# The last chunk's inverse butterflies reordered and written to other tiles, the third layer's normalisation split in two, and the butterfly scratch tile moved

## The chip, the cores and the metric

The kernel runs as one program on one core of a Trainium2 chip. The metric is the device time of one execution in microseconds; the figure before is the median of three executions. A profiled execution of the same program, taken separately, gives the trace.

## The reference

Four layers are applied to `x` of 2048 rows (time) by 640 columns (channels), each behind a layer norm without weights and each added to `x`:

```python
x = A_u
x = x + _A_ref(_layernorm(x), A_re, A_im, B_re, B_im, C_re, C_im, log_dt, Dskip)   # layer "a"
x = x + _B_ref(_layernorm(x), wq, wk, wv, wo)                                     # layer "b"
x = x + _A_ref(_layernorm(x), A_re, ...)                                          # layer "c"
x = x + _B_ref(_layernorm(x), wq, ...)                                            # layer "d"
```

`_A_ref` is a long convolution: a kernel of 2048 taps for each channel is built from complex exponentials, and the convolution is done by FFT over 4096 points, product and inverse FFT, plus a skip term. `_B_ref` is attention with 32 query heads of 20 columns and one shared key and value head, softmax over 2048 keys, and an output projection.

## The kernel before, in words

`tile_layers` (L1351) runs the parts in order: `kgen` builds the convolution's taps and stores them in DRAM (`kd`); `conv_layer("a", True)`, `attn_layer("b")`, `conv_layer("c", False)`, `attn_layer("d", out)`. The activations `x` stay in SBUF as 16 tiles `tau` = 0 to 15 of 128 rows and 640 columns. The engines are TensorE (PE), ScalarE (ACT), VectorE (DVE), GpSimd (POOL) and SyncE (SP, which issues most DMAs); each works through its own queue in order.

**A convolution layer.** The 640 channels are cut into five chunks `c` of 128. For one chunk the work is:

- `normals` or `normal` (L760 to L770): ACT writes the normalised chunk into the tile `xn`, one instruction of 128x128 for each `tau` and copy. `norm` (L694, with `rstd` and `root`) works the scales and shifts out of the mean and variance in `mv`: some ten tiny DVE instructions around one square root on ACT.
- `raw` (L562) or `dense` (L594): PE multiplies by the tables `wf`. There are four groups `t` of 128-wide products, each into its own PSUM tile `z`, and ACT copies each into the chunk's spectrum tile `A` (16 slots of 256 columns). `dense` does a first butterfly inside the products, by a moving operand of 256 columns and by negated copies in `xn` (24 ACT instructions instead of 16). With `raw` this first butterfly is left to DVE: `halve` (L580), two instructions of 128x2048. `halved` (L820) says how many chunks go by `raw`: one in layer a, two in layer c.
- `fft8` (L104): the forward butterflies, 16 DVE instructions between `A` and the scratch tile `B`.
- The product with the taps' spectrum `kh`: `spread` (L840), eight DVE instructions and four accumulating DMAs issued by POOL; for the last chunk `product` (L778), six DVE instructions with the scratch `R`. `load_spectrum` (L709) fetches `kh` by a DMA on SP's queue.
- `halve` and `fft8` again for the inverse, then `inverse` (L792): PE multiplies the slots by the tables `wi`, in four groups `g` of four `tau` each, group `g` holding the `tau` with `tau % 4 == FIRST[g]`, `FIRST = (0, 2, 1, 3)`. `residual` (L810) adds the result to `x`, on DVE or, for chunks 0 and 3, on ACT. The results `y` go through two PSUM banks in turn, so the third group waits until the first one's residual has read its bank; `turn` (L899) issues residual `g` and then `inverse` `g + 2`.

Chunks overlap: while DVE does one chunk's inverse, PE prepares the one after the next. Inside `conv_layer` the order on PE, ACT and DVE is the order in which the code is written (`manual_schedule`), and `weave` puts pieces of one list between the pieces of another. In layer a, `kernel_spectra` (L718) first runs the five chunks of taps through `raw`, `whole` and a store to `kh`. In layer a's last chunk, pieces of `attn_weights` (L928) on ACT and PE are woven between the DVE instructions. Then `stats_last` and `norm_part` finish the norm for the attention layer that follows.

**An attention layer.** `_attn` (L997) normalises `x`, transposes it and makes queries, keys and values; `main_loop` (L1150) goes through 4 x 8 x 16 steps of scores (L1187), exponentials on ACT (L1191) and values (L1201). Output projections are slipped in between (L1261), their sums into `x` and the statistics for the next norm done on DVE (`add`, `stats`). After the last step `normalize_last` (L1234) makes the tile `on`, and the last projections of the last four `tau` (all with `tau % 4 == 3`) use it with the weights `wol` (L1307). Here the order on PE and ACT is written by hand, that on DVE is left to the planner.

**Where tiles lie.** A pool gives each tile its place by the order of creation. The convolution's pool, the pools of an attention layer and `kgen`'s pool start at the same address, right behind `x` and its small companions. So a tile may only be written once the last reader of whatever lay there before is done. In KiB from that start: `kgen`'s two staging tiles `kst`, from which the taps are stored to DRAM, lie at 0 to 16. In the convolution pool, `B` is created in `conv_setup` and lies at 0 to 16, `R` at 16 to 24. In layer c `xn` lies at 24 to 36, `A1` at 36 to 52, `kh` at 52 to 68, `wi` from 68. An attention layer's pools have `kt`, `vt` and others at 0 to 15, the query tiles at 15 to 27, `wo` at 27 to 40, `wol` at 40 to 42, the exponentials `pt` at 42 to 66, two tiles `on` at 66 to 70, and the projection's staging tiles `ot` at 74 to 94.

Of the kernel before, what the change touches and what calls it, by code (L numbers as in the profile page):

```python
# [21 lines left out]
P = 128  # L22
# [124 lines left out]

def weave(calls, between):

    for i in range(len(calls) + 1):  # L150
        for n, call in between:
            if n == i or (i == len(calls) and n > i):
                call()
        if i < len(calls):
            calls[i]()


class Net:
# [7 lines left out]
    def setup(self, ctx):  # L166
# [8 lines left out]
        self.mv = self.xp.tile([P, 16, 2], F32, name="mv")  # L175
# [355 lines left out]
    def conv_setup(self, ctx):  # L531
# [3 lines left out]
        self.cvp = ctx.enter_context(tc.tile_pool(name="cvp", bufs=1, reuse_waits="tile"))  # L535

        self.B = self.cvp.tile([P, 16, 256], F32, name="B")
# [20 lines left out]
    def spectrum(self, nm, k):  # L558
        tag = f"A{k}" if k < 3 else "kh"
        return self.cvp.tile([P, 16, 256], F32, tag=tag, bufs=1, name=f"A{nm}")  # L560

    def raw(self, xn, nm, k):  # L562
# [4 lines left out]
        for t in range(4):  # L567
# [12 lines left out]
    def halve(self, A, pieces=1):  # L580
# [3 lines left out]
        for i in range(pieces):  # L584
# [5 lines left out]
    def whole(self, A, sg, pieces=1):  # L590

        return self.halve(A, pieces) + fft8(self.nc, A, self.B, sg, low=self.B[:, 8:16])
# [32 lines left out]
    def stats(self, t):  # L625
# [5 lines left out]
        nc.vector.bn_aggr(self.mv[:, t], st.rearrange("p a b -> p (a b)"))  # L631
# [62 lines left out]
    def norm(self, nm):  # L694
        rs = self.xp.tile([P, 16], F32, tag="rs", bufs=2, name=f"rs{nm}")
        nmr = self.xp.tile([P, 16], F32, tag="nmr", bufs=2, name=f"nmr{nm}")
        self.rstd(self.xp, self.mv, rs, nmr, 16)
        return rs, nmr

    def rstd(self, pool, mv, out, nmr, n):  # L700

        nc = self.nc
        ve = pool.tile([P, n], F32, tag="ve", bufs=2, name="ve")
        sq = pool.tile([P, n], F32, tag="sq", bufs=2, name="sq")
        nc.vector.tensor_scalar(ve, mv[:, :, 1], EPS, None, ALU.add)
        self.root(ve, sq, out)
        nc.vector.scalar_tensor_tensor(nmr, mv[:, :, 0], -1.0, out, op0=ALU.mult, op1=ALU.mult)
# [10 lines left out]
    def kernel_spectra(self):  # L718
# [5 lines left out]
        ktl = cv.tile([P, 24, DC], F32, tag="xn", name="ktl")  # L724
        ks += [kts[:, c] for c in range(3)] + [ktl[:, 0:16]]
# [12 lines left out]
    def conv_layer(self, nm, first):  # L738
# [4 lines left out]
        B = self.B  # L743
        tt = nc.vector.tensor_tensor
        with tc.manual_schedule(engines={mybir.EngineType.PE, mybir.EngineType.Activation,
                                         mybir.EngineType.DVE}):
            rs, nmr = self.norm(nm)
            rsm = self.xp.tile([P, 16], F32, tag="rsm", bufs=1, name=f"rsm{nm}")
# [644 lines left out]
```

## Time and profile before

| what | us |
|---|---|
| median of 3 executions (3016.51 to 3018.91) | 3018.55 |
| profiled execution, its own time | 3015.11 |
| its span in the trace | 3013.3 |
| layer a, first product with the taps to last product (L574 to L804) | 301.2 to 613.8 |
| attention b, first scores to last projection (L1187 to L1261) | 734.2 to 1692.8 |
| layer c, first normalising instruction to last product (L761 to L804) | 1698.3 to 1927.9 |
| attention d, first scores (L1187) | 2048.1 |

A row of the timeline gives start, duration, engine, line and operation, the tiles (written <- read, buffer numbers left out, so `Ak` are the spectra of the taps, `Aa` and `Ac` those of layers a and c), the count of merged instructions, and in brackets how long the engine had stood idle and who ended that. A row of the windows gives for each stretch its length, the busy time of PE, weight loads, DVE, ACT and POOL with instruction counts, then PE's granted clock as a share of full speed, the DMA share and GB/s. A row of the waits gives who waited for whom: total us, times, longest. The chain that ended last covers only attention d, so the stages around the change are read from timelines.

### The profile page before, as it was taken

Reading aid. Unit: us, or ns where it says so; the run is one execution under the profiler, and the core shown is the slowest. Engines: PE = TensorE matmul, PEld = TensorE weight load, DVE = VectorE, ACT = ScalarE, POOL = GpSimd, SP = SyncE. Lnnn points to the kernel's source line nnn. Section 1 sums busy time; section 2 is a strip of 40 time slices with the busy share of each in tenths; the row PEclk is TensorE's granted clock in tenths of the full one; section 3 lists DMA queues with packets and bytes.
Section 4 is the critical chain, followed back from the end, with each engine's and each line's share of the span. In section 5 each row is a group of like instructions: output and inputs, shape, how many; then the busy total and the mean of one; then the engine's idle time right before and its main releaser. Section 6 shows DMA issues by size and latency. Waiting matters only on the chain. (4 is left out here: it accounts for less than half of the span.)

```text
span 3013.3 us, 52501 instructions
## 1 busy us (share of the span) xinstructions
PE 2787.7 (93%) x21712; PEld 1275.9 (42%) x21712; DVE 1371.8 (46%) x1774; ACT 2429.1 (81%) x2910; POOL 86.6 (3%) x149
## 2 busy tenths in 40 slices
PE   2776999898999999999999898798999999999999
PEld 0333988775232323333333687673223333333323
DVE  7999899942122232322232499721222223232222
ACT  5888343444999999999999534238999999999997
POOL 0001001000000000000000011000000000000000
PEclk9855999999999999999999999899999999999999
DMA  6113555433200000100000256131000100110100
GB/s 145 34 21 106 170 168 112 103 114 112 81 22 25 22 27 20 28 23 24 25 22 20 87 112 152 35 131 56 24 25 22 43 22 26 38 28 22 42 19 23
DMA packets 126001, 175.60 MB, mean 58 GB/s; under 512 B 59461, under 2 KB 81989, under 8 KB 122133
## 3 DMA queue, kind: packets, MB, share of 16 engines
q1 hardware_dynamic: 102680, 137.70, 15.8%
q0 software_dynamic: 21104, 33.45, 5.5%
q8 instruction: 175, 2.87, 0.4%
q10 hardware_dynamic: 1968, 0.98, 0.1%
q14 instruction: 74, 0.60, 0.1%
HBM read 95.22 MB, written 48.04 MB: 48 GB/s over the span
## 5 line engine op out<-in xcount | busy, mean ns | idle before, releaser
L1191 ACT ACTIVATE pt<-scb 128x1024 f32<-128x1024 f32 x1024 | 942.1, 1120 | 7.0 <-PE scb L1187 5.7
L1191 ACT ACTIVATE pt<-scd 128x1024 f32<-128x1024 f32 x1024 | 942.2, 1117 | 6.3 <-PE scd L1187 4.9
L1201 PE MATMUL pod<-pt,vt 128*32 128x512 f32 x4096 | 546.5, 606 | 4.4 <-DVE on L1218 0.5
L1201 PE MATMUL pob<-pt,vt 128*32 128x512 f32 x4096 | 546.4, 605 | 4.4 <-DVE on L1218 0.5
L1187 PE MATMUL scb<-qpb,kt 62*128 62x512 f32 x2048 | 385.6, 451 | 6.6 <-PEq L1136 5.9
L1187 PE MATMUL scd<-qpd,kt 62*128 62x512 f32 x2048 | 385.7, 451 | 5.8 <-DVEq L1136 5.4
L1187 PEld LDWEIGHTS scb<-qpb,kt 62*128 62x128 f32 x2048 | 166.1, 185 | 402.2 <-ACT pt L1191 392.3
L1187 PEld LDWEIGHTS scd<-qpd,kt 62*128 62x128 f32 x2048 | 166.0, 185 | 401.3 <-ACT pt L1191 391.9
L1249 DVE TENSOR_TENSOR x<-pyd,x 128x320 f32<-128x320 f32 x146 | 71.8, 492 | 560.8 <-PE pyd L1261 560.8
L1249 DVE TENSOR_TENSOR x<-pyb,x 128x320 f32<-128x320 f32 x146 | 71.8, 492 | 547.4 <-PE pyb L1261 547.4
L1221 DVE RECIPROCAL rc<-rc 128x512 f32<-128x512 f32 x62 | 207.9, 3353 | 2.1
L1201 PEld LDWEIGHTS pod<-pt,vt 128*32 128x32 f32 x4096 | 80.6, 108 | 177.9 <-issue 159.9
L1201 PEld LDWEIGHTS pob<-pt,vt 128*32 128x32 f32 x4096 | 80.6, 108 | 177.5 <-issue 159.5
L608 PE MATMUL za<-xna,wf 128*128 128x256 f32 x512 | 114.0, 384 | 7.7 <-ACT xna L761 7.7
L608 PEld LDWEIGHTS za<-xna,wf 128*128 128x128 f32 x512 | 97.9, 192 | 23.1 <-ACT xna L761 9.7
L1261 PE MATMUL pyb<-wo,ot 128*32 128x320 f32 x1168 | 105.3, 432 | 0.0
L1261 PE MATMUL pyd<-wo,ot 128*32 128x320 f32 x1168 | 105.3, 432 | 0.0
L804 PE MATMUL yc<-Ac,wi 128*128 128x128 f32 x640 | 77.6, 284 | 21.2 <-DVE Ac L114 21.2
L608 PE MATMUL zc<-xnc,wf 128*128 128x256 f32 x384 | 87.4, 390 | 4.6 <-ACT xnc L761 4.5
L804 PEld LDWEIGHTS yc<-Ac,wi 128*128 128x128 f32 x640 | 77.2, 201 | 25.7 <-issue 12.8
L804 PE MATMUL ya<-Aa,wi 128*128 128x128 f32 x640 | 76.2, 281 | 10.0 <-DVE Aa L114 10.0
L610 ACT ACTIVATE Aa<-za 128x1024 f32<-128x1024 f32 x16 | 16.4, 1023 | 83.1 <-PE za L608 83.1
(323 smaller groups left out, 3093.2 us busy)
## 6 DMA issues: line engine op xcount, KB each, us to landing
Akh<-kh SPq DMA_DIRECT2D x10, 2048.0 KB
kh<-Ak SPq DMA_DIRECT2D x5, 2048.0 KB
qhd<-qh SPq DMA_DIRECT2D x40, 256.0 KB
qld<-ql SPq DMA_DIRECT2D x40, 256.0 KB
qpb<-qhd SPq DMA_DIRECT2D x256, 40.0 KB
qpd<-qhd SPq DMA_DIRECT2D x256, 40.0 KB
ot<-on SPq DMA_DIRECT2D x216, 40.0 KB
wf<-in_c_wf POOLq DMA_DIRECT2D x16, 512.0 KB, 8.3
```

What stands on the lines that cost most here:

```text
L608: nc.tensor.matmul(zv[:, :, c, kk], self.wf[:, t + 4 * h, j, c, kk], x, start=(n == 0), stop=(n == 3))
L610: nc.scalar.activation(A.rearrange("p (o s) d -> p o s d", o=2)[:, :, 2 * t : 2 * t + 2], z.rearrange("p (c o e) -> p o c e", c=2, o=2), A ...
L804: nc.tensor.matmul(y[:, s * DC : (s + 1) * DC], self.wi[:, t, j, c_, kk], v[:, 2 * t + c_, kk], start=(i == 0 and not whole), stop=(i == 3 ...
L1187: nc.tensor.matmul(sc[:, 512 * par : 512 * par + 512], kt[rows, 128 * t : 128 * t + 128], qps[nb, hg, pr][rows], start=True, stop=True)
L1191: nc.scalar.activation(pt, sc, AF.Exp, scale=SCALE)
L1201: nc.tensor.matmul(po[32 * j : 32 * j + 32], vt[:, t], pts[step, j // 2][:, 512 * (j % 2) : 512 * (j % 2) + 512], start=(t == 0), stop=(t ...
L1221: nc.vector.reciprocal(rc, rc)
L1249: nc.vector.tensor_tensor(xh, py, xh, ALU.add)
L1261: nc.tensor.matmul(py[j : j + m], o[:, 128 * i + j : 128 * i + j + m], w[:, 320 * half : 320 * half + 320], start=start, stop=stop)
```

## The change

1. `fft8_last` takes the place of the last two butterflies of `product` and of `fft8` for the last chunk, in both convolution layers: again 24 DVE instructions of the same sizes with the product, but those of the even slots first, and these results go to `kh`'s tile (now `K`), with `R` as scratch, instead of into `A`. `inverse` takes groups 0 and 1 from `K`, groups 2 and 3 from `A`.
2. `mv` becomes two tiles: one for the 12 `tau` with `tau % 4 != 3`, one for the other four. `norm` works on one of them. For layer c the first part is issued in attention b's `main_loop`, right behind `normalize_last`; the second inside layer c's first chunk. That chunk takes its groups in the order `FIRST`: eight normalising instructions ahead, and the others inside `raw` (`ahead`).
3. `halved` is 2 in layer a too: chunk 1 goes by `raw` and `halve` instead of `dense`.
4. Places. `B` is created by `butterflies`. In layer a that is behind the staging of the taps: `kh`'s tile lies at 0 to 16 KiB now, `R` at 16 to 24, `wi` at 24 to 56, `xn` at 56 to 68, `B` at 68 to 84. In layer c the order is `B` 0 to 16, `A1` 16 to 32, `A2` 32 to 48, `xn` 48 to 60, `R` 60 to 68, `kh` 68 to 84, `wi` 84 to 116.

```diff
+def fft8_last(nc, A, B, R, K):
...
+    tt(A[:, 0:8], B[:, 0:8], B[:, 8:16], ADD)
+    tt(R[:, 0:4], A[:, 0:4], A[:, 4:8], ADD)
+    tt(R[:, 4:8], A[:, 0:4], A[:, 4:8], SUB)
+    tt(K[:, 0:2], R[:, 0:2], R[:, 2:4], ADD)
+    tt(K[:, 8:10], R[:, 0:2], R[:, 2:4], SUB)
+    tt(K[:, 4:14:9], R[:, 4:6], R[:, 7:5:-1], SUB)
+    tt(K[:, 12:4:-7], R[:, 4:6], R[:, 7:5:-1], ADD)
+    tt(A[:, 8:16], B[:, 0:8], B[:, 8:16], SUB)
+    tt(B[:, 8:12:3], A[:, 8:10], A[:, 13:11:-1], SUB)
+    tt(B[:, 10:8:-1], A[:, 8:10], A[:, 13:11:-1], ADD)
+    tt(B[:, 0:2], A[:, 10:15:4], A[:, 11:16:4], ADD)
+    tt(B[:, 2:4], A[:, 10:15:4], A[:, 11:16:4], SUB)
+    tt(B[:, 12:16:3], B[:, 2::-2], B[:, 1:4:2], SUB)
+    tt(B[:, 14:12:-1], B[:, 2::-2], B[:, 1:4:2], ADD)
+    f0, f2, f1, f3s = B[:, 8:10], B[:, 10:12], B[:, 12:14], B[:, 15:13:-1]
+    stt(A[:, 2:4], f1, RT_HALF, f0)
+    stt(A[:, 10:12], f1, -RT_HALF, f0)
+    stt(A[:, 6:16:9], f3s, -RT_HALF, f2)
+    stt(A[:, 14:6:-7], f3s, RT_HALF, f2)
...
-        self.mv = self.xp.tile([P, 16, 2], F32, name="mv")
+        self.mv = [self.xp.tile([P, 12, 2], F32, name="mv0"), self.xp.tile([P, 4, 2], F32, name="mv1")]
+        self.rn = None
...
         self.cvp = ctx.enter_context(tc.tile_pool(name="cvp", bufs=1, reuse_waits="tile"))
-
+        if self.rn is None:
+            self.placed["k3"] = self.spectrum("k3", 3)
+
+    def butterflies(self):
         self.B = self.cvp.tile([P, 16, 256], F32, name="B")
...
-    def raw(self, xn, nm, k):
+    def raw(self, xn, nm, k, order=range(4), ahead=lambda t: None):
...
-        for t in range(4):
+        for t in order:
+            ahead(t)
...
+    def norm(self, nm, g):
...
+        nc, n = self.nc, (12, 4)[g]
...
         ktl = cv.tile([P, 24, DC], F32, tag="xn", name="ktl")
+        self.butterflies()
...
+        if not first:
+            self.butterflies()
...
-            rs, nmr = self.norm(nm)
...
+            if first:
+                self.norm(nm, 0)
+                self.norm(nm, 1)
             self.norm_next(nm)
             if first:
                 self.kernel_spectra()
-            R = self.scratch(nm)
+            else:
+                for c in range(2):
+                    self.placed[f"{nm}{c}"] = self.spectrum(f"{nm}{c}", c + 1)
+                self.placed["xn"] = self.cvp.tile([P, 24, DC], F32, tag="xn", bufs=1, name=f"xn{nm}0")
+            R, B = self.scratch(nm), self.B
...
-                    (m(B, 1), m(B, 1), R, ALU.add),
-                    (A[:, 0:8], B[:, 0:8], B[:, 8:16], ALU.add),
-                    (A[:, 8:16], B[:, 0:8], B[:, 8:16], ALU.subtract))]
+                    (m(B, 1), m(B, 1), R, ALU.add))]
...
-            halved = 1 if first else 2
+            halved = 2
...
+                if c == 0 and not first:
+                    for t in FIRST[:2]:
+                        group(t)
+
+                    def ahead(t):
+                        if t == FIRST[0]:
+                            group(FIRST[2])
+                        elif t == FIRST[1]:
+                            self.norm(nm, 1)
+                            group(FIRST[3])
+
+                    return self.raw(xn, f"{nm}{c}", 1, FIRST, ahead)
...
-                    weave(product(A, khs.pop(c)) + fft8(nc, A, B, +1), late)
+                    K = khs.pop(c)
+                    weave(product(A, K) + fft8_last(nc, A, B, R, K), late)
...
-                ys = [inverse(c, g, A) for g in range(2)]
+                ys = [inverse(c, g, K if c == NCH - 1 else A) for g in range(2)]
...
             on = normalize_last()
+            if out is None:
+                self.norm("c", 0)
```

`group(t)` writes the four normalised tiles of one class, as the loop before did.

74 lines of the change are left out of this document (44 added, 30 removed).

## Prediction

> **What bounds the kernel now.** I read the page first, for the shape of the whole.
>
> ```profile
> span 3013.3 us, 52501 instructions
> ...
> PE 2787.7 (93%) x21712; PEld 1275.9 (42%) x21712; DVE 1371.8 (46%) x1774; ACT 2429.1 (81%) x2910; POOL 86.6 (3%) x149
> ```
>
> PE's 93% says little here: the attention loops fill it, and the change touches none of their instructions. A loop that starts earlier ends earlier, so a microsecond won ahead of one is won at the end. What counts is which engine hands on last in four places: layer a's start, its middle, the border from attention b to layer c, and layer c's end. For these I read the timelines. Layer a's start:
>
> ```profile
> 315.76 1.02 ACT L576 ACTIVATE Ak<-zk 128x1024 f32<-128x1024 f32 x1 [2.55 <-PE zk L574]
> 319.12 0.69 DVE L587 TENSOR_TENSOR B<-Ak 128x512 f32<-128x512 f32 x1 [12.87 <-DMA kd<-kst]
> ...
> 330.06 1.02 ACT L576 ACTIVATE Ak<-zk 128x1024 f32<-128x1024 f32 x1 [2.55 <-PE zk L574]
> ...
> 335.78 2.29 DVE L587 TENSOR_TENSOR B<-Ak 128x2048 f32<-128x2048 f32 x1
> ```
>
> DVE's first write to `B` waits 12.87 us, not for its input but for the DMA that stores the taps out of `kst`: `B` lies on those tiles. Then DVE is behind ACT and stays so. Layer a's middle, DVE and PE:
>
> ```profile
> 374.39 14.72 PE L574 MATMUL za<-xna,wf 128*128 128x128 f32 x128 [1.49 <-ACT xna L761]
> ...
> 392.53 29.15 PE L608 MATMUL za<-xna,wf 128*128 128x256 f32 x126 [0.46 <-ACT xna L761]
> ...
> 398.77 0.69 DVE L587 TENSOR_TENSOR B<-Aa 128x512 f32<-128x512 f32 x1
> ...
> 437.23 2.29 DVE L587 TENSOR_TENSOR B<-Aa 128x2048 f32<-128x2048 f32 x1 [1.77 <-DMA Aa<-Akh]
> ...
> 445.36 1.29 DVE L114 TENSOR_TENSOR Aa<-B 128x512 f32<-128x512 f32 x2
> ...
> 452.39 1.02 PE L797 MATMUL ya<-x,ident 128*128 128x512 f32 x2
> ...
> 475.68 2.29 DVE L587 TENSOR_TENSOR B<-Aa 128x2048 f32<-128x2048 f32 x1 [2.72 <-issue]
> ...
> 501.82 2.36 DVE L114 TENSOR_TENSOR B<-Aa 128x1024 f32<-128x1024 f32 x2 [1.37 <-ACT Aa L610]
> ...
> 543.74 2.36 DVE L114 TENSOR_TENSOR B<-Aa 128x1024 f32<-128x1024 f32 x2 [1.98 <-ACT Aa L610]
> ```
>
> and in the waits from 398 to 560 us:
>
> ```profile
> DVE x L815 <- PE ya L804: 2.9, 8, 0.5
> ```
>
> DVE carries this stage with few pauses, and most of them are waits for PE: the copies of the dense chunks (1.37, 1.98) and the residuals (2.9). PE and DVE are nearly level. The border:
>
> ```profile
> 1680.82 0.36 SPq L711 DMA_DIRECT2D Akh<-kh  x1
> ...
> 1688.29 4.47 PE L1261 MATMUL plb<-wol,onl 128*128 128x320 f32 x16
> 1689.57 0.89 DVE L1249 TENSOR_TENSOR x<-plb,x 128x320 f32<-128x320 f32 x2 [3.93 <-PE plb L1261]
> ...
> 1692.79 4.01 SPq L555 DMA_DIRECT2D wi<-in_c_wi  x8
> ...
> 1696.24 0.21 DVE L631 BATCH_NORM_AGGREGATE mv<-st 128x2 f32<-128x12 f32 x1
> ...
> 1698.32 6.26 ACT L761 ACTIVATE xnc<-x,nmrc,rsc 128x128 f32<-128x128 f32 x16 [1.42 <-DVE rsmc L750]
> ...
> 1698.87 16.80 PE L574 MATMUL zc<-xnc,wf 128*128 128x128 f32 x128 [6.11 <-ACT xnc L761]
> ...
> 1715.71 1.02 ACT L576 ACTIVATE Ac<-zc 128x1024 f32<-128x1024 f32 x1 [2.55 <-PE zc L574]
> ```
>
> PE ends at 1692.76 (1688.29 + 4.47) and waits 6.11 us while the statistics of the last `tau`, the norm's ten tiny steps and the first normalised tiles follow one another. Then its 128 products take 16.80 us where the same shape took 14.72 in layer a. Layer c's end:
>
> ```profile
> 1902.96 4.49 DVE L779 TENSOR_TENSOR Ac<-B 128x2048 f32<-128x2048 f32 x2
> 1907.49 3.56 DVE L114 TENSOR_TENSOR B<-Ac 128x1024 f32<-128x1024 f32 x4
> 1910.97 1.29 DVE L114 TENSOR_TENSOR Ac<-B 128x512 f32<-128x512 f32 x2
> ...
> 1911.80 16.16 PE L804 MATMUL yc<-Ac,wi 128*128 128x128 f32 x128 [9.58 <-DVE Ac L114]
> ...
> 1918.44 0.69 DVE L815 TENSOR_TENSOR x<-yc,x 128x512 f32<-128x512 f32 x1
> ...
> 1928.00 0.69 DVE L815 TENSOR_TENSOR x<-yc,x 128x512 f32<-128x512 f32 x1 [1.17 <-PE yc L804]
> ```
>
> Here PE has always started on the first slots that are ready: at 1911.80, while the butterflies run on to 1918.44.
>
> **The change part by part.** *B off the staging tiles.* Chunk 0's work from 319.12 to 335.78 is 16.66 us, of which the four halved pieces can follow ACT's copies; the last copy ends at 316.78, so chunk 0 is done by about 329.4 and chunk 1 starts when its last copy ends, at 330.06 + 1.02 = 331.08 instead of 335.78: 4.7 us earlier, and DVE keeps that through to 398.77, since from there it is the later one. The `kh` tile that now lies on `kst` is first written several chunks on. Layer a's norm in two parts adds ten tiny DVE steps in the 12.87 us wait: nothing, 2 us if that cover were gone.
>
> *Chunk 1 by raw.* PE is relieved of 29.15 - 14.72 = 14.4 us, ACT of eight instructions; DVE gets two halving instructions, 4.5 us (2 x 2.29, overlapping a little). DVE is the path, so this is a cost of 4.5, unless waits go. The wait of 1.77 goes, since DVE comes 4.5 us later after the DMAs that it waits for were issued. PE does chunk 2's dense products up to some 14 us earlier and can begin chunk 0's inverse when DVE's first slots are there: 0.65 after 445.36, less the 1.9 us that DVE leads by then (4.7 - 4.5 + 1.77), about 444 where 452.39 stood. So its lead on DVE grows by some 8 us: the wait of 1.37 and half of the 2.9 go (chunk 1's four residuals). [...] Gone: 1.77 + 1.37 + 1.45 + 1.1 + 0.3 = 6.0. Layer a: 4.7 - 4.5 + 6.0 = 6.2 us earlier. Bounds: 1.5 (the start gains nothing: 6.0 - 4.5) to 7.5 (the 0.9 and some of the 2.4 go too). DVE's own work is next late there.
>
> *The border.* Twelve `tau` are normalised ahead. Their ten DVE steps fit into the wait of 3.93 before 1689.57; the square root stands behind ACT's last exponential; `xn` now lies on `pt` buffers only, so ACT can write twelve tiles (about 0.39 us each by 6.26/16, 4.7 us) before PE ends. PE goes on at 1692.76 without a pause and takes 14.72: the last copy starts at 1707.5, not 1715.71. The last four `tau` have time: statistics at 1696.45, square root behind the first copy (about 1697.5), its chain and four tiles by about 1701; PE asks for them after three quarters of 14.72, at 1703.8. In front of ACT's queue the second and third copies wait less than 1 us for that. Gain 8.2 us; bounds 6.1 (the pause alone) and 8.5. What loses: `kh`'s load. At 68 KiB it lies on the last `on`, so it moves from 1680.82 to where `wi` stood, 1692.8, with `wi` queued behind it on SP. DVE needs it here:
>
> ```profile
> 1729.29 2.36 DVE L857 SCALAR_TENSOR_TENSOR Rc<-Ac,Akh 128x1024 f32<-128x1024 f32 x2
> ```
>
> or 8.2 earlier, 1721. By shape `kh` has 2.1 MB, `wi` 4.2, and their two stretches moved
>
> ```profile
> 1680.00:1688.00 8.00, 8.00 (x35) 5.24 (x28) 4.77 (x4) 0.90 (x1) 0.00 (x0) 1.00 0.73 262
> 1692.00:1704.00 12.00, 5.89 (x28) 5.32 (x27) 5.93 (x23) 5.89 (x16) 0.00 (x0) 0.72 0.86 326
> ```
>
> 262 and 326 GB/s; 6.3 MB at 262 take 24 us, to 1717. Hidden; price nothing.
>
> *The even half first.* In layer a's end:
>
> ```profile
> 599.38 14.46 PE L804 MATMUL ya<-Aa,wi 128*128 128x128 f32 x128
> ```
>
> PE comes straight from the weight pieces and does the four groups without a pause: an earlier half finds PE busy and gains nothing. The memsets for attention b that had to wait for `B` wait for group 1's reading of `K` now, some 3 us longer; their readers come well after that.
>
> In layer c's end the first result in `K` comes after one instruction of 2.25 (half of 4.49), two of 1.2 (3.56 holds two of these and two of 0.65) and one of 0.65, 5.3 us after 1902.96, at 1908.3: PE starts 3.5 us earlier. But group 2 needs the bank that residual 0 frees, and that residual still stands behind all the butterflies, which are as many as before: 1918.44 + 0.69 = 1919.1. Groups 0 and 1 take half of 14.46 and the 1.7 us that the slow start costs today (16.16 - 14.46), so they are done at 1917.2; PE then stands for 2 us and ends at 1919.1 + 7.2 = 1926.4 instead of 1927.96, 1.5 us earlier if its clock holds. It may not:
>
> ```profile
> 423.93 0.70 PE L608 MATMUL za<-xna,wf 128*128 128x256 f32 x2 [2.26 <-ACT xna L761]
> ...
> 1734.14 29.81 PE L608 MATMUL zc<-xnc,wf 128*128 128x256 f32 x128 [2.26 <-ACT xnc L761]
> ```
>
> ```profile
> 424.00:453.00 29.00, 28.54 (x130) 24.65 (x131) 27.02 (x36) 11.35 (x25) 2.90 (x3) 1.00 0.70 143
> ...
> 1734.00:1738.00 4.00, 3.78 (x9) 2.59 (x10) 4.00 (x4) 4.00 (x12) 2.37 (x3) 0.57 0.13 17
> ...
> 1912.00:1915.00 3.00, 3.00 (x15) 3.00 (x16) 2.96 (x6) 0.00 (x0) 0.00 (x0) 0.50 0.00 0
> ```
>
> The granted clock is 0.50 after the long wait, and 0.57 from 1734 on after PE had stood for only 2.26 us; behind the same pause at 423.93 it was 1.00. Another slow start costs 1.7 and puts the end 0.2 later than now. I take 0.5 us of gain, between the two and nearer to the slow one, since the 1734 pause is the nearest row. [...]
>
> Sum: 6.2 + 8.2 + 0.5 = 14.9 us. The profiled execution's 3015.11 (1.8 around the span) becomes 3000.2; it stood 3.4 under the median of 3018.55, which becomes 3003.6.
>
> **The rivals.** *Layer a gives nothing.* DVE pays 4.5 and PE's waits turn into waits for the accumulating DMAs, of which the 1.77 and 2.72 are examples; for it speaks that DVE has no slack there, against it that more than half of its waits name PE or ACT (1.37, 1.98 and 2.9 of 10.7). Total 8.7: 3009.9.
>
> *The early norm isn't early.* In `main_loop` only PE's and ACT's order is written by hand; if the planner puts the ten DVE steps behind the last sums, the square root stays behind 1696.45 and the border gains nothing. The 3.93 us hole ahead of the sums speaks against it. Total 6.7: 3011.9.
>
> *Slower: `kh` lands late.* One mechanism: 6.3 MB on one queue from 1692.8. It costs nothing until 1721, eats everything from 1735.9 on, that is below 146 GB/s. The page's slices show such rates:
>
> ```profile
> GB/s 145 34 21 106 170 168 112 103 114 112 81 22 25 22 27 20 28 23 24 25 22 20 87 112 152 35 131 56 24 25 22 43 22 26 38 28 22 42 19 23
> ```
>
> At 112 it lands at 1749, 28 us late: 13 us slower, 3031.6. Against it stand the 262 and 326 of the same two loads; a slice averages over 75 us.
>
> **How the numbers follow.** Forecast 0.70, layer a nothing 0.14, the norm not early 0.09, `kh` late 0.04, and 0.03 that these gains cancel in something unseen. A measurement tells about 0.2%, 6 us. Faster takes the first two and most of the third (6.7 is close to 6): 0.91; same 0.05; slower 0.04. The forecast's own range, from its bounds (layer a 1.5 to 7.5, border 6.1 to 8.5, end -0.2 to 1.5: 7.4 to 17.5), is 3001 to 3011; to hold 8 in 10 with the first two rivals' times (3009.9, 3011.9) and the 3.4 us between executions, 2999.5 to 3012.
>
> **What would show it.** In the changed trace: DVE's first halving no later than 309 with no DMA wait; raw's last copy in layer c some 14.8 us after PE's last projection, clock at 1.00 between; chunk 1 of layer a at about 14.7 us on PE; the product with `kh` without a DMA wait. At layer c's end PE should start 5.3 us after the halving, yet stand before group 2 until the first residual: if it doesn't, that part is worth more. Wrong would be a border gain under 6 or a layer a that ends less than 4 us earlier relative to its start.

## The result, and the profile after

| | before | after |
|---|---|---|
| median of 3 executions, us | 3018.55 | 2999.59 (2997.73 to 2999.66) |
| profiled execution, us | 3015.11 | 2999.59 |
| its span, us | 3013.3 | 2997.8 |

The ratio is 0.9939, with an interval from 0.9925 to 0.9952. 3003.6 was forecast, in a range from 2999.5 to 3012. The medians lie 19.0 us apart and the two profiled executions 15.5; the 3.4 between them is the distance by which the profiled execution before stood under its own median. The sum of the prediction, 14.9, stands against the 15.5. The measured 2999.59 lies 0.1 above the lower end of the range.

```profile
span 2997.8 us, 52536 instructions
...
PE 2777.6 (93%) x21712; PEld 1269.2 (42%) x21712; DVE 1378.1 (46%) x1794; ACT 2426.4 (81%) x2904; POOL 86.7 (3%) x149
```

The page's first lines again tell next to nothing: the same 93% on PE. The stages tell it, each measured between two rows that both traces have (the last product of layer a, the last projection of attention b, the fourth copy of layer c's chunk 0, the first of the last chunk's butterflies, the last product of layer c):

| stage | before | after | earlier by | forecast |
|---|---|---|---|---|
| start to the end of layer a's last product | 613.84 | 610.76 | 3.1 | 6.2 |
| then to the end of the last projection | 1078.92 | 1078.66 | 0.3 | 0 |
| the border: then to the start of the fourth copy | 22.95 | 14.33 | 8.6 | 8.2 |
| then to the first of the last butterflies | 187.25 | 186.67 | 0.6 | 0 |
| then to the end of layer c's last product | 25.00 | 22.83 | 2.2 | 0.5 |
| then to the end of the span | 1085.34 | 1084.55 | 0.8 | 0 |

The sum came out nearly as forecast, two of its three terms did not. The timeline of the kernel after, layer a first (PE and DVE):

```profile
300.96 16.21 PE L618 MATMUL zk<-Rk,wf 128*128 128x128 f32 x128 [1.07 <-DMA Rk<-kd]
...
307.60 0.68 DVE L631 TENSOR_TENSOR B<-Ak 128x512 f32<-128x512 f32 x1
...
332.56 2.29 DVE L631 TENSOR_TENSOR B<-Ak 128x2048 f32<-128x2048 f32 x1 [1.80 <-ACT Ak L620]
...
445.73 6.46 PE L860 MATMUL ya<-Aa,wi 128*128 128x128 f32 x32 [5.54 <-DVE Aa L114]
...
468.48 29.05 PE L652 MATMUL za<-xna,wf 128*128 128x256 f32 x126 [0.46 <-ACT xna L818]
...
474.22 2.29 DVE L631 TENSOR_TENSOR B<-Aa 128x2048 f32<-128x2048 f32 x1 [1.65 <-issue]
...
540.55 2.36 DVE L114 TENSOR_TENSOR B<-Aa 128x1024 f32<-128x1024 f32 x2 [1.99 <-ACT Aa L654]
...
596.30 7.31 PE L860 MATMUL ya<-Akh,wi 128*128 128x128 f32 x64
603.45 7.31 PE L860 MATMUL ya<-Aa,wi 128*128 128x128 f32 x64
```

and in the waits from 398 to 560 us:

```profile
DVE x L871 <- PE ya L860: 2.7, 7, 0.5
```

In the kernel before, the row that matches the one at 468.48 was:

```profile
473.27 27.46 PE L608 MATMUL za<-xna,wf 128*128 128x256 f32 x126 [0.46 <-ACT xna L761]
```

The first halving starts at 307.60 without a DMA wait, as forecast. But chunk 1's halving is only 3.2 us earlier than the 335.78 of before, not 4.7, because the first 128 products with the taps took 16.21 us where they took 14.53 before (granted clock from 302 to 304 us: 0.50, against 1.00): the copies came late. Further on PE now waits 5.54 us for chunk 0's first inverse slots, where it had been the late one, and then takes 6.46 us over a group that otherwise takes 3.73 (granted clock from 446 to 450 us: 0.50). Behind a pause of 1.83 us its next dense products took 29.05 us, 1.6 more than before, again at a granted clock of 0.50 for a part (469 to 471 us). So PE lost 4.3 us after the pause of 5.54. Of DVE's waits 1.77 and 1.37 are gone and 2.72 became 1.65, but 1.98 stands (1.99), and the residuals' 2.9 became 2.7. The last row pair shows the even half coming from `kh`'s tile, without a pause and without a gain in layer a.

The border, in the timeline:

```profile
1677.57 0.21 ACT L736 ACTIVATE sq0c<-ve0c 128x12 f32<-128x12 f32 x1
...
1683.11 4.72 ACT L818 ACTIVATE xnc<-x,nmr0c,rs0c 128x128 f32<-128x128 f32 x12 [5.33 <-DVE rsm0c L756]
1684.95 4.47 PE L1334 MATMUL plb<-wol,onl 128*128 128x320 f32 x16
1689.26 14.45 PE L618 MATMUL zc<-xnc,wf 128*128 128x128 f32 x128
1689.45 0.36 SPq L762 DMA_DIRECT2D Akh<-kh  x1
...
1703.75 1.02 ACT L620 ACTIVATE Ac<-zc 128x1024 f32<-128x1024 f32 x1 [2.55 <-PE zc L618]
...
1717.32 2.36 DVE L929 SCALAR_TENSOR_TENSOR Rc<-Ac,Akh 128x1024 f32<-128x1024 f32 x2
```

PE goes from the projections (1684.95 + 4.47) to the products with no pause between, and these take 14.45 us instead of 16.80 (granted clock from 1689 to 1704 us: 1.00, where it was 0.57 from 1696 to 1704 before). The square root stands right behind the last exponential. `kh` is fetched from 1689.45 on, and its first reader at 1717.32 waits for no DMA.

Layer c's end, in the timeline:

```profile
1890.42 2.29 DVE L157 TENSOR_TENSOR Ac<-B 128x2048 f32<-128x2048 f32 x1
...
1895.81 10.30 PE L860 MATMUL yc<-Akh,wi 128*128 128x128 f32 x64 [6.49 <-issue]
...
1902.57 0.69 DVE L871 TENSOR_TENSOR x<-yc,x 128x512 f32<-128x512 f32 x1 [0.33 <-PE yc L860]
...
1904.71 2.48 DVE L160 SCALAR_TENSOR_TENSOR Ac<-B 128x512 f32<-128x512 f32 x4
1905.94 7.31 PE L860 MATMUL yc<-Ac,wi 128*128 128x128 f32 x64
```

PE starts 5.39 us after 1890.42, where it started 8.84 after 1902.96: 3.45 earlier, as forecast (3.5). The surprise is the third row: residual 0 runs at 1902.57, ahead of the four last butterflies, so PE goes on with group 2 at once.

### The profile page after: what moved, and what is told of

It is laid out like the page before. It is cut to its first block, busy times and chain, and to the rows that moved or that the text cites. A ratio compares the mean times of both kernels' runs of the same rounds, so it can differ in the third digit from the quotient of the medians.

```text
span 2997.8 us, 52536 instructions
## 1 busy us (share of the span) xinstructions
PE 2777.6 (93%) x21712; PEld 1269.2 (42%) x21712; DVE 1378.1 (46%) x1794; ACT 2426.4 (81%) x2904; POOL 86.7 (3%) x149
## 5 line engine op out<-in xcount | busy, mean ns | idle before, releaser
L1264 ACT ACTIVATE pt<-scd 128x1024 f32<-128x1024 f32 x1024 | 942.1, 1115 | 5.8 <-DMA qpd<-mxd 3.9
L652 PE MATMUL za<-xna,wf 128*128 128x256 f32 x384 | 87.4, 390 | 5.0 <-ACT xna L818 5.0
L860 PE MATMUL ya<-Aa,wi 128*128 128x128 f32 x576 | 71.8, 289 | 15.5 <-DVE Aa L114 15.5
L1291 DVE COPY on<-pod 128x512 f32<-128x512 f32 x31 | 21.4, 691 | 134.6 <-PE pod L1274 120.6
L1291 DVE COPY on<-pob 128x512 f32<-128x512 f32 x31 | 21.4, 691 | 133.0 <-PE pob L1274 110.0
L443 PE MATMUL pe<-kg,tm 48*128 48x512 bf16 (+1 forms) x120 | 60.1, 603 | 23.9 <-ACT m L451 15.4
L652 PEld LDWEIGHTS za<-xna,wf 128*128 128x128 f32 x384 | 74.8, 196 | 16.8 <-ACT xna L818 6.2
```

The source lines that it names most:

```text
L443: nc.tensor.matmul(pe[:, 512 * h : 512 * h + 512], grp(tm, u, par, rows), kg[0:rows, col : col + 512], start=True, stop=True)
L652: nc.tensor.matmul(zv[:, :, c, kk], self.wf[:, t + 4 * h, j, c, kk], x, start=(n == 0), stop=(n == 3))
L860: nc.tensor.matmul(y[:, s * DC : (s + 1) * DC], self.wi[:, t, j, c_, kk], v[:, 2 * t + c_, kk], start=(i == 0 and not whole), stop=(i == 3 ...
L1264: nc.scalar.activation(pt, sc, AF.Exp, scale=SCALE)
L1291: nc.vector.tensor_copy(on, po)
```

## The experiments

Each kernel was executed at least five times beside the kernel before. The interval of one ratio is about 0.14% to each side, 4 us, as much as most of the parts; so the parts are read from the stages of the traces, and the ratio only says whether the whole agrees.

**1. `B` on the staging tiles again** (layer a's places as before):

```diff
-            self.placed["k3"] = self.spectrum("k3", 3)
+            self.butterflies()
...
-        self.butterflies()
```

> The changed kernel with layer a's tiles placed as before, `B` on the staging tiles again. The first halving should wait about 12.9 us for the taps' store once more, with its start at about 319. Theory from the two traces: moving `B` was worth 3.2 us (chunk 1's first halving went from 335.78 to 332.56, no more, because the first tap products ran at half clock), and it is carried to layer a's end: 3002.8 us, layer a 3.2 us later than changed. The prediction's term: 4.7 us, 3004.3. Rival, layer a's start does not set its end (PE or the accumulating DMAs do): under 1 us, 2999.6 to 3000.6.

Median 3003.74, ratio 0.9961 (0.9948 to 0.9975). The timeline:

```profile
318.64 0.69 DVE L631 TENSOR_TENSOR B<-Ak 128x512 f32<-128x512 f32 x1 [10.58 <-DMA kd<-kst]
...
335.29 2.29 DVE L631 TENSOR_TENSOR B<-Ak 128x2048 f32<-128x2048 f32 x1
```

The wait is back and chunk 1's halving is 2.7 us later than in the changed kernel, yet layer a's last product ends at 611.46, only 0.7 later. In that stage neither theory's size was met, and the rival's under 1 us came nearest: the wait of 1.99 is 1.03 here, and chunk 1's residuals hardly wait. But PE's speed has a part in that: in this execution its first inverse group took 5.42 us instead of 6.46 and its next dense products 27.46 instead of 29.05 (those of the changed kernel at the granted clock of 0.50 given above), 2.6 us less. So the 0.7 is `B`'s price in this pair of traces, and, by estimate from these, up to 2 more at equal speed. The median lies 2.8 and 4.2 us above the two of the changed kernel (2999.59, and 3000.90 in run 9), which one interval hardly tells from nothing.

**2. Chunk 1 of layer a by `dense` again**

```diff
-            halved = 2
+            halved = 1 if first else 2
```

> The changed kernel with layer a's chunk 1 by `dense` again. Theory from the traces: raw there gave about nothing, 4.5 us of DVE paid and about as much of waits gone: 2999 to 3000.6, layer a's end within 1 us of the changed kernel. The prediction's term: 6.0 of waits gone for 4.5 paid, so 1.5 us slower without it, 3001.1. Rival, raw is a loss there because PE is not the late one: 1 to 3 us faster without it, 2996.6 to 2998.6, with the waits of 1.77 and 1.37 back.

Median 3007.80, ratio 0.9968 (0.9956 to 0.9980). Layer a's last product ends at 615.59: 4.8 us later than in the changed kernel, and 1.8 later than in the kernel before. All three sizes fell, the prediction's in its direction right. In the timeline (PE, then DVE):

```profile
375.74 14.72 PE L618 MATMUL za<-xna,wf 128*128 128x128 f32 x128 [1.49 <-ACT xna L818]
...
504.54 2.36 DVE L114 TENSOR_TENSOR B<-Aa 128x1024 f32<-128x1024 f32 x2 [5.62 <-ACT Aa L654]
```

DVE starts as early as in the changed kernel (chunk 1's halving at 332.46) and waits it all away: 5.62 us in this row, where 1.37 stood before. PE is the path here, with pauses of 0.5 to 2.3 us for ACT's normals alone between the first products with the taps and chunk 0's inverse, and it runs 1.35 us later than before (375.74 against 374.39): the copy behind the first 128 products with the taps ended 17.4 us after they began, 15.6 before. So the new theory: before, PE bound layer a's first half, not DVE. That PE had no wait for DVE from its first product with the taps at 301.20 to 556 us in the trace before, and has one of 5.54 us now, speaks for it too. The early start alone is worth nothing, `raw` relieves PE and makes DVE the bound, and only then does the start count. End of layer a's last product: 613.84 with neither, 615.59 with `B` moved alone, 611.46 with `raw` alone, 610.76 with both. These four are single executions: the 1.8 that `B` alone seems to lose is PE's speed (1.35 at the start, where the granted clock was 0.50 from 301 to 304 us against 1.00 in the kernel before, and 1.7 in dense products that took 29.15 instead of 27.46, less 1.1 won in a later group), not a price of `B`.

**3. The old last butterflies**

```diff
-                    weave(product(A, K) + fft8_last(nc, A, B, R, K), late)
+                    weave(product(A, K) + fft8(nc, A, B, +1), late)
...
-                ys = [inverse(c, g, K if c == NCH - 1 else A) for g in range(2)]
+                ys = [inverse(c, g, A) for g in range(2)]
```

(with the two halvings back in `product`)

> The changed kernel with the old last butterflies (`product` with its two halvings, `fft8`, all four groups out of `A`) in both layers. Theory from the traces: layer a's end unchanged, layer c's end 2.2 us longer because residual 0 no longer gets in ahead of the odd half and PE starts later: 3001.8; the stretch from the last product's end to the last `y` product 2.2 us longer. The prediction's term: 0.5 us, 3000.1. Rival, PE's early start buys nothing since the half clock eats it: 0, 2999.6.

Median 3003.13, ratio 0.9952 (0.9939 to 0.9966). Layer a's last product ends at 610.89, 0.1 later: nothing there, as was expected. Layer c's end takes 26.22 us (1890.75 to 1916.97), 3.4 more than in the changed kernel:

```profile
1899.60 17.37 PE L862 MATMUL yc<-Ac,wi 128*128 128x128 f32 x128 [10.01 <-DVE Ac L114]
```

The same 128 products, begun as long after the halving, took 16.16 before, so 1.2 of the 3.4 lie in their speed in this execution, and 2.2 in the change. The prediction's 0.5 was too small; the rival that nothing is gained fell.

**4. The norm's first part at the head of layer c**

```diff
-            if out is None:
-                self.norm("c", 0)
...
-            if first:
-                self.norm(nm, 0)
+            self.norm(nm, 0)
+            if first:
                 self.norm(nm, 1)
```

> The changed kernel with the first part of layer c's norm moved back to the head of the convolution layer; the two parts, the order of the groups and the places of the tiles stay. Theory: the early issue is what took the pause away, so PE's pause of about 6 us behind the last projection comes back with the slow products after it: 8 to 8.6 us slower than changed, 3007.6 to 3008.2. Rival A, the places do it (`xn` off the tiles `on`, so that ACT may write while PE still projects) and the planner pulls the norm ahead anyway: under 2 us, 2999.6 to 3001.6. Rival B, half and half: the 12 normalised early save the normals but not the chain, 3 to 5 us slower, 3002.6 to 3004.6.

Median 3004.77, ratio 0.9961 (0.9948 to 0.9975). The border keeps its 14.33 us (1692.71 to 1707.04), so the planner did pull the norm ahead, as rival A had it. But it went too far ahead, in ACT's timeline:

```profile
1524.16 1.28 ACT L736 ACT_TABLE_LOAD   x1
1525.46 0.21 ACT L736 ACTIVATE sq0c<-ve0c 128x12 f32<-128x12 f32 x1
1525.69 1.28 ACT L1264 ACT_TABLE_LOAD   x1
```

The square root sits among the exponentials, 150 us early, with a table load on each side. From the first scores of attention b to its last projection it takes 963.42 us instead of 958.65: 4.8 us lost in a loop that ACT bounds (its exponentials fill 942.1 us of it in the profile before). The three rows are 2.8 of that; 1.8 are ACT's next two waits for scores (0.76 and 1.05). The explicit place behind the last exponential is what keeps the norm from doing that, and so the run does not measure what that place is worth at the border, only that the border's gain does not hang on it.

**5. The norm whole again**

```diff
-        return (1, t // 4) if t % 4 == 3 else (0, 3 * (t // 4) + t % 4)
+        return 0, t
...
-        nc, n = self.nc, (12, 4)[g]
+        nc, n = self.nc, 16
```

(called once, at the head of layer c)

> The changed kernel with layer c's norm in one part again over all 16 `tau`, so that it needs the last sums of attention b; the order of the groups and the places of the tiles stay. Theory: splitting the norm is what took the pause and the slow products away, so the stretch from the last projection to the fourth copy of chunk 0, 14.33 us in the changed kernel, goes back to 22 to 23 us: 8 to 8.6 us slower, 3007.6 to 3008.2. Rival: the places of the tiles and the order of the groups brought part of it (`xn` off the tiles `on`), and the stretch is 16 to 20 us: 2 to 6 us slower, 3001.6 to 3005.6.

Median 3007.51, ratio 0.9972 (0.9962 to 0.9983). The timeline:

```profile
1683.06 4.47 PE L1331 MATMUL plb<-wol,onl 128*128 128x320 f32 x16
1693.66 16.77 PE L618 MATMUL zc<-xnc,wf 128*128 128x128 f32 x128 [6.14 <-ACT xnc L816]
...
1710.46 1.02 ACT L620 ACTIVATE Ac<-zc 128x1024 f32<-128x1024 f32 x1 [2.55 <-PE zc L618]
```

The pause (6.14) and the slow products (16.77) are back, the border takes 22.93 us: 8.6 more than in the changed kernel, with the places and the order of the groups kept. Without the split the places and the order bring nothing, so the term hangs on the split, and the rival fell. Whether the split would bring it without the new places was not run.

**6. The first residual behind all the butterflies**

```diff
-        turn(0)
+            turn(0)
```

(so that it falls under the order written by hand)

> The changed kernel with the first residual of the last chunk put into the order written by hand, behind all the butterflies. Theory from the trace: in the changed kernel residual 0 got in ahead of the last four butterflies, which is why PE never stood before group 2; put behind them it comes at about 1907 instead of 1902.57, group 2 starts at about 1907.3 instead of 1905.94, and layer c's end is 1.3 us later, 3000.9; layer a's end does not move. Rival one: group 2 needs the first slots of the odd half anyway, so at most 0.3 us is lost. Rival two, the prediction's own step: PE stands for 2 us and its clock falls to half for the second two groups, 3 us or more.

Median 3000.40, ratio 0.9948 (0.9935 to 0.9962). The timeline of layer c's end (DVE, PE):

```profile
1907.32 1.28 DVE L871 TENSOR_TENSOR x<-yc,x 128x512 f32<-128x512 f32 x2
1908.06 7.41 PE L860 MATMUL yc<-Ac,wi 128*128 128x128 f32 x64 [0.67 <-DVE x L871]
```

PE now stands 0.67 us before group 2, which takes 7.41 us and so is hardly slower than in the changed kernel (7.31); the stage takes 23.76 us (1891.71 to 1915.47) instead of 22.83: 0.9 lost where 1.3 was expected. The rivals of 0.3 and of 3 fell. This is the kernel that the prediction had in mind, and it gains 1.2 on the 25.00 of before.

**7. PE kept busy in layer a's wait**

```diff
+                    if first and c == 0:
+                        w = self.ps2("warm")
+                        for _ in range(40):
+                            nc.tensor.matmul(w[:, 0:P], self.ident, self.ident, start=True, stop=True)
```

(behind chunk 0's inverse butterflies; nobody reads `w`)

> The changed kernel with 40 products of the identity with itself added on PE in layer a, into a free PSUM tile, in the 5.54 us in which PE waits for chunk 0's first inverse slots. Theory: that wait halves the granted clock, the first inverse group takes 6.46 us instead of 3.73, and PE is the last engine from there to chunk 4's transform; with the clock kept at 1.00 layer a ends 2 to 2.7 us earlier, 2996.9 to 2997.6. Rival: DVE takes over at once, under 1 us, 2998.6 to 2999.6. Second rival: the added products don't hold the clock or make the first group late, no gain or up to 1 us slower.

**12. The same with 24 products** instead of 40

> The changed kernel with the 24 added products in layer a's wait alone. Theory: 40 of them took 9.1 us and put off the first inverse group by about 1.5 us, 24 take 5.5 and do not; chunk 4's transform starts at about 536.5 instead of 538.6 to 539.9 for the same start, layer a ends at 605 to 606.3 instead of 608.5 to 608.9 (1.7 later in each case where the first products with the taps run slowly), and the rest of the kernel is unchanged: 2.5 to 3.5 us faster than the changed kernel, a ratio to the kernel before of 0.9932 to 0.9936. Rival: layer a's gain does not come out at the end of the kernel, as in the run with 40, because the stages behind layer a take one or two us more: a ratio of 0.9942 to 0.995.

Medians 3000.32 and 3001.32, ratios 0.9949 (0.9936 to 0.9963) and 0.9951 (0.9938 to 0.9965). The 40 products took 9.09 us and put the first inverse group at 445.78, 114.7 us after chunk 1's first halving of the taps; with the 24 it is 113.2, as in the changed kernel. The timeline of the kernel with 24 (its row counts 48 for the 24 products):

```profile
437.79 5.52 PE L973 MATMUL warm<-ident 128*128 128x128 f32 x48
...
444.68 3.84 PE L860 MATMUL ya<-Aa,wi 128*128 128x128 f32 x32 [0.51 <-DVE Aa L114]
...
464.80 27.46 PE L652 MATMUL za<-xna,wf 128*128 128x256 f32 x126 [0.45 <-ACT xna L818]
...
537.00 2.36 DVE L114 TENSOR_TENSOR B<-Aa 128x1024 f32<-128x1024 f32 x2 [1.05 <-ACT Aa L654]
```

and its waits from 398 to 560 us:

```profile
DVE x L871 <- PE ya L860: 1.5, 4, 0.5
```

With PE kept busy, the group takes 3.84 instead of 6.46 and the next dense products 27.46 instead of 29.05, the wait of 1.98 falls to 1.05 and the residuals' 2.9 to 1.5: these are the prediction's numbers (0.9, which is 1.98 less the 1.1 of its sum, and half of 2.9). From chunk 1's first halving of the taps to layer a's last product it takes 274.2 (40) and 275.0 us (24), against 277.0 to 278.3 in six executions without such products (the changed kernel twice, runs 3, 4, 5 and 6). Part of that spread arises behind it, in a later group; to the start of the last chunk's products it takes 176.6 us in both, against 179.0 to 179.4 in the six. So the theory held for layer a, with 2.4 us. Run 8, which has the 40 products too, is no such case: its first group takes no longer (3.73), but comes 3.2 us late behind the added products, the dense products take 29.09, and layer a takes 278.7. For the end of the kernel no gain came out, as the second rival of run 7 and the rival of run 12 had it: the medians lie where the changed kernel's do, 2999.59 and 3000.90. In the profiled execution with 24, layer a ends 2.1 us earlier than in run 9, and that went in the next stage: from the first transposes of attention b to its first scores 122.87 us passed instead of 120.48 there and 118.95 in the first trace, PE's clock being, in the windows of the two kernels (24, then the changed one):

```profile
614.00:620.00 6.00, 4.91 (x15) 2.49 (x14) 2.95 (x3) 5.39 (x7) 0.00 (x0) 0.50 0.00 0
```

```profile
618.00:624.00 6.00, 4.65 (x23) 2.85 (x22) 2.95 (x3) 5.64 (x8) 0.00 (x0) 0.96 0.00 0
```

In eleven other executions without products added there, that stage took 118.8 to 120.9 us. Whether the 122.87 is chance or follows from the earlier end isn't settled by these runs.

**8. Also ahead of the taps' last piece**, 40 products into the tile `pk`

```diff
+                if u == len(units) - 1:
+                    for _ in range(40):
+                        nc.tensor.matmul(PK[u][:, 0:P], self.ident, self.ident, start=True, stop=True)
```

> As the run before, and another 40 such products on PE in the 6.68 us in which it waits for the last piece of the taps' generation. Theory: the first 128 products with the taps took 16.21 us in the changed kernel against 14.53 before only because the clock was still at half when they began; kept busy ahead, PE has full clock there, chunk 1's first halving comes at about 330.7 instead of 332.56, and layer a ends 1.9 us earlier still: 2995.0 to 2995.7. Rival: the gain of 1.9 does not reach layer a's end, which the DMAs or DVE set: as the run before.

Median 3005.66, ratio 0.9964 (0.9950 to 0.9977): slower, for a reason that neither theory had. PE's timeline:

```profile
292.89 12.14 PE L478 MATMUL pk<-ident 128*128 128x128 f32 x80 [4.75 <-ACT kst L492]
...
306.89 5.29 PE L621 MATMUL zk<-Rk,wf 128*128 128x128 f32 x45
```

The tile was not free until 292.89 and the products took 12.14 us, so the first product with the taps started 5.9 us late (its row is cut off by the end of the view, at 312 us). The run says nothing on the clock's price there.

**9. The changed kernel once more**

> The changed kernel once more, as it is, as a yardstick beside the two runs that follow it on the same chip. Theory: the executions of one kernel differ by up to 5 us because the granted clock rises and falls at moments that are not tied to the program; so its ratio to the kernel before should fall into the interval of the first measurement, 0.9925 to 0.9952, while single stages (the first products with the taps, layer c's end, the start of the projections) take one of two or three durations. Rival: the stages keep the durations of the first trace (16.21 us for the first 128 products with the taps, 118.6 us from the first transposes of layer d to its first scores), and the differences between runs lie elsewhere, in the attention loops.

Median 3000.90 (2999.61 to 3003.95), ratio 0.9946 (0.9932 to 0.9960): inside the first interval. In this execution the first products with the taps ran at full speed (granted clock from 302 to 304 us: 1.00):

```profile
301.63 14.53 PE L618 MATMUL zk<-Rk,wf 128*128 128x128 f32 x128 [1.65 <-DMA Rk<-kd]
```

14.53 where the first trace had 16.21 (at 0.50 there), and layer a's last product ends at 608.51 instead of 610.76. The attention loop of layer d, first scores to last product, differs less: 959.2 against 958.1. So the rival is wrong in its first half, that the stages keep their durations, and the theory stands: single stages jump.

**10 and 11. PE kept busy among the projections too**: as in 12, and 8 products behind the third transpose and 4 ahead of the first projection of each attention layer; 11 also 18 products ahead of the taps' last piece, in another tile

> The changed kernel with PE kept busy in three kinds of waits by products of the identity whose results nobody reads: 24 (about 5.4 us) in layer a ahead of the first inverse group, and in both attention layers 8 and 4 among the first transposes and ahead of the first projection. Theory: the half clock in these places costs PE time on the path; the first inverse group takes 3.73 us instead of 6.46 and starts no later, layer a ends 3 to 4.5 us earlier than in the changed kernel with the same clock at the start, and each attention layer's stretch from the first transposes to the first scores is at its shortest, 118.6 to 119: 4 to 6 us faster than the changed kernel, 2993.5 to 2995.5. Rival: the gain of layer a is there and is lost again behind it, since DVE and ACT set the projections' start: 0 to 2 us, 2997.5 to 2999.5.

> As the run before, and 18 such products in PE's 6.68 us wait ahead of the last piece of the taps' generation, in a free PSUM tile. Theory: with full clock at the first products with the taps these take 14.5 us in each execution, not 16.2 in some: 0 to 1.9 us faster than the run before, and the runs lie closer together. Rival: the wait is too short for the added products, they push the last piece of the taps back, and the first product with the taps starts after 302 instead of 301: up to 3 us slower than the run before.

Medians 3002.74 and 3007.01, ratios 0.9954 (0.9940 to 0.9969) and 0.9964 (0.9950 to 0.9978): both misses, slower than the changed kernel where a gain was expected. The added products did not run in the wait but behind it, in PE's timeline of run 10:

```profile
1914.46 1.29 PE L1118 MATMUL ptd<-ident,x 128*128 128x128 f32 x4 [3.20 <-ACT x L1109]
1915.54 3.62 PE L1122 MATMUL ptd<-ident 128*128 128x128 f32 x16
```

The 8 took 3.62 us, where 8 of the 24 in run 12 took 1.84 (a third of 5.52); the granted clock was 0.77 on the mean from 1910.71 to 1916.71 us and 0.67 in the 6 us behind. They lie on the path: the stretch to the first scores took 123.45 us instead of 118.61. In run 11 the first 128 products with the taps were slow all the same (their copy ended 17.1 us after they began, against 15.6 in run 9; granted clock from 302 to 304 us: 0.50). No version that was tried beats the changed kernel by more than the runs differ.

## Why the prediction was nearly right, step by step

- **Layer a's start.** The wait of 12.87 us for the taps' store went as told, but "DVE keeps that through" failed: before, PE was the late engine there, not DVE, and run 2 shows that `B`'s move alone gives nothing. That PE and DVE were "nearly level" was true; the step that took DVE as the path was not. The 4.7 were 3.2 in the first trace, since the first products took 16.21 us, and 4.2 in run 9, where they took 14.53.
- **Chunk 1 by `raw`.** The mechanism was right in that the waits 1.77 and 1.37 are gone and PE's lead grew. The relief of PE, 14.4, was read off a row with a slow part: the 126 products of 29.15 us take 27.46 behind 425.09 us, at a granted clock of 1.00 (424 to 453 us; it was 0.50 from 393 to 395 us). The 6.0 us of waits were 4.4. The 0.3 in its sum leaves 2.4 of the 2.72, a size that no run shows as a DMA's landing; the wait fell to 1.65. The 1.1 leaves 0.9 of the 1.98, but that stayed (1.99; 1.05 in run 12), and most of the 2.9 did. They stayed because the lead turned into a pause of 5.54 us, and behind it PE lost 2.7 us in one group and 1.6 in the next dense products, both at a granted clock of 0.50 for a part (446 to 450 and 469 to 471 us). Runs 7 and 12, where PE is kept busy there, lose neither and show just the numbers that were forecast for these two. Layer a together: 3.2 - 4.5 + 4.4 = 3.1 for 6.2 (2.8 relative to its start), less than the 4 that the prediction named as a sign of being wrong. Run 9 has 5.3, but 1.5 of that is one group behind a later wait (5.19 us against 6.69 before) and no gain of the change. With PE kept busy, layer a ended 7.4 (run 12) and 8.6 us (run 7) earlier than before, 0.6 and 1.4 of it in that later group.
- **The border.** 8.6 for 8.2, each step as told: no pause, a granted clock of 1.00 from 1689 to 1704 us, the four late `tau` in time, `kh` hidden. Run 5 ties it to the split of the norm.
- **The even half.** Nothing in layer a, as forecast. In layer c the step that failed is "that residual still stands behind all the butterflies": `turn(0)` of layer c's last chunk lies outside the hand-written order, the planner moves it ahead, and PE has no second pause. Run 6, which puts it where the prediction had it, measures 1.2 of gain, near the 1.5 that held "if its clock holds"; the speed did hold, with 7.41 us for the 64 products against 7.31, over the 0.67 us that PE stood (not 2, since the first two groups took 10.3 us and not 9). The other 0.9 is the residual's place. The 0.5 was thus mis-sized twice.
- **The rivals.** Layer a gave half, not nothing; that its waits would turn into waits for the accumulating DMAs was not seen, those shrank. The early norm was early. `kh` was in time.
- **The sum.** 14.9 against 15.5 is in good part luck: 3.1 too much in layer a, 0.4 too little at the border and 1.7 at layer c's end, and 1.6 in stages that the change was not expected to move. The 0.6 of layer c's middle can be PE's slow chunk at 1734 before: its 128 products took 29.81 us there and 28.62 in the changed kernel (1722.18 to 1750.80), and DVE's wait for the last chunk's copies fell from 1.36 to 0.59. The rest is no more than executions differ by. The median itself came 4.0 under the forecast, at the edge of the range: 0.6 is this difference, and 3.4 that the median before lay above its profiled execution and the one after did not.

## To carry to other kernels

Two engines that are "nearly level" must both be followed through as the path before a microsecond is credited to either: here an earlier DVE was worth nothing alone, a lighter PE 2.4 us, and both together 3.1 in the first traces. When a change turns an engine's lead into a pause, look at what that engine does first after the pause, not only at the wait that went. And an instruction that a planner may move is worth checking for both directions: it put one residual in a better place than the source says, and a square root in a worse one.

## What the runs showed of the hardware

PE's granted clock falls from 1.00 to 0.50 in spells whose length the instructions alone do not set: 6.8 and 10.2 us in the first two here. The windows of 1 us around the two ends of one spell, behind layer c's last products, in the changed kernel and then in run 7:

```profile
1915.30:1916.30 1.00, 0.00 (x0) 0.00 (x0) 0.96 (x9) 0.00 (x0) 0.00 (x0) 0.64 0.00 0
...
1922.30:1923.30 1.00, 0.23 (x1) 0.17 (x2) 1.00 (x2) 1.00 (x3) 0.00 (x0) 0.95 0.00 0
```

```profile
1911.30:1912.30 1.00, 0.00 (x0) 0.00 (x0) 0.69 (x7) 0.33 (x2) 0.00 (x0) 0.80 0.00 0
...
1921.30:1922.30 1.00, 1.00 (x4) 0.50 (x3) 0.00 (x0) 0.55 (x1) 0.00 (x0) 0.58 0.00 0
```

A mean of 0.64 over a window that begins at 1.00 and ends at 0.50 puts the fall at 1915.58, one of 0.95 the rise at 1922.40 (estimates from these windows; those on their outer sides show 1.00, the six between them 0.50): a spell of 6.8 us. In run 7 it is 1911.90 to 1922.14, 10.2 us, for the same instructions. Layer a's spell in the changed kernel, from

```profile
444.00:446.00 2.00, 0.27 (x1) 0.27 (x2) 2.00 (x4) 0.00 (x0) 0.00 (x0) 0.61 0.00 0
...
450.00:452.00 2.00, 2.00 (x14) 2.00 (x14) 1.97 (x5) 0.00 (x0) 0.00 (x0) 0.69 0.00 0
```

444.44 to 451.24, is 6.8 us again. The next one there, from

```profile
467.00:469.00 2.00, 1.22 (x3) 0.80 (x4) 2.00 (x5) 2.00 (x6) 0.00 (x0) 0.83 1.20 174
...
471.00:473.00 2.00, 2.00 (x9) 1.66 (x9) 1.57 (x3) 2.00 (x7) 0.00 (x0) 0.82 1.16 168
```

468.32 to 471.72, is 3.4 us. From the rise at 451.24 to the next fall at 468.32 it is 17.1 us. What sets these lengths the runs don't show. Where PE worked in a spell it lost about half of that time: 2.7 of 5.5 us (445.73 to 451.24, 6.46 us instead of 3.73), 1.6 of 3.2 (468.48 to 471.72, 29.05 instead of 27.46) and 1.7 of 3.5 (300.96 to 304.48, 16.21 instead of 14.53; the windows from 301 to 304 us show 0.50, the one from 304 to 305 shows 0.76). The spell from 444.44 began while PE stood, and cost it only in the part that was left at 445.73. There are several such places in this kernel, and the five executions of run 9 spread from 2999.61 to 3003.95; whether the spells are all of that spread was not followed up. The clock fell behind short pauses too: the 0.57 at 1734 before came behind a pause of 2.26 us, and the fall at 468.32 behind pauses of 1.83 and 0.46. Behind the same 2.26 at 423.93 before the clock stayed at 1.00 (424 to 453 us), and behind the same 1.83 and 0.45 in run 12 (the row at 464.80) the products took the 27.46 us that they took before at 1.00. So in these rows the length of the pause does not decide it; what does was not shown, since no run moved a pause alone. A change of one or two microseconds in such a kernel is seen stage by stage in several traces, not in one time.
